# Value products in the two halves of the array's rows, and the first group's maxima in four PSUM banks

## The chip, the cores and the metric

The kernel runs as one program on one core of a Trainium2 chip. The metric is the device time of one execution in microseconds (us). Three runs of the kernel before gave 850.44, 850.53 and 852.36 us, median 850.53 us.

Engine names are those of the profile: PE is TensorE's matrix multiply, PEld its weight load, DVE is VectorE, ACT is ScalarE, POOL is GpSimd, SP is SyncE, which here only issues DMAs.

## The reference

The input x has 2048 rows of 512 numbers. Two branches are computed from it and mixed by a gate for each row:

```
g = sigmoid(sum(x * gate_w))
q, k, v = split(x @ wqkv)                       # 32 heads of 16
s = (q @ k^T) / 4, masked to 0 <= query - key < 256
a = (softmax(s) @ v) @ wo
b = (silu(x @ w_gate) * (x @ w_up)) @ w_down    # inner width 1792
out = g * a + (1 - g) * b
```

A query sees itself and the 255 keys before it. In blocks of 128 this means that a block of keys is seen by its own block of queries and by the two that follow, so by up to 384 queries.

## The kernel before, in words

The kernel holds most operands as a high and a low part (float32r) and multiplies three products (high x high, high x low, low x high) where one would do in full precision. The attention is worked group by group: a group `g` is 4 heads, and there are 8 groups.

**Start.** x is loaded and split, the values of all heads are projected in `vproj2`, and the queries and keys of groups 0 and 1 are projected. While the last 12 blocks of values are projected, the running of `first` puts in the maxima of group 0: `stage1` computes the scores of one head for one block of queries on PE (L264, heads in pairs: head `j` of a pair lies in array rows 0 to 63 or 64 to 127) and a custom DVE instruction adds the mask and takes the maximum over the keys (L266). The scores of `stage1` come from the pool `ps1`, which has two PSUM buffers (banks) handed out in turn.

**The attention loop.** Step `t` stands for group `g` and block `i` of 128 (16 steps for a group). In each step there are four parts `hd` = 0 to 3. Each part puts on PE, in this order: one score product of `stage1` for the next group (L264), one of `stage2` for this group (L301), and six products of `lanes` (L216), which are projections for a later group or early parts of the feed-forward branch. `stage2` scores go through the exponential on ACT (L303), from the pool `ps2` of two banks, into the tiles `pt`, which POOL then masks (L305, L308). From step 112 on (the last group), there is no `stage1` any more, and `stage2` runs two heads at once in parts 0 and 2.

At each fourth step, in part 1, stands a *value site*: `av` multiplies the exponentials of 4 blocks of queries (a chunk `c` of 512) with the values (L319), `evac` transposes the result out of PSUM on DVE (L329), and `finish` divides by the sum and transposes back over the next steps. There are 32 sites, `d` = 1 to 32. In `av` each product has all 128 keys of a block on the array's rows and 32 columns for a head, so the four heads of a group stand side by side in the four column groups. It runs over up to 384 queries. It sums in one bank taken from the pool `pp`.

At every second value site (steps with `i` = 8 or 0, so even `d` up to 28) `put_max` stands ahead of `av`: it transposes the maxima on PE (L276, a bank from `ps1`), DVE copies them negated into `mt` (L278), and SP moves them into the query tile, so that the score product of `stage2` subtracts them.

**The order of the work** is written out: each engine executes its instructions in the order in which the code above issues them. A PE instruction that waits for a bank holds up all that stands behind it on PE.

**The feed-forward stage** follows. For chunk `c` and slice `n` of the inner width, `hidden` takes the two inputs (kept in DRAM as `raws` and loaded as `got`, or computed on PE at L633), applies silu on ACT (L636) and multiplies on DVE (L637); `halved` splits the product into high and low (ACT L64, DVE L67); `step` multiplies with `w_down` (L82 to L84). The loop at the end of the stage keeps `halved` one slice behind `hidden`, and `step` two behind.

Of the kernel before, what the change touches and what calls it, by code (L numbers as in the profile page):

```python
# [9 lines left out]
F32 = mybir.dt.float32  # L10
# [6 lines left out]
P = 128  # L17
# [16 lines left out]
def gated_mix(ctx, tc, xT, xn, wqk, wv, wo, wgu, wd, gw, out):  # L34
# [43 lines left out]
    def mm3(ps, pairs, start=True, stop=True):  # L78

        n = len(pairs)  # L80
        for i, ((lh, ll), (rh, rl)) in enumerate(pairs):
            nc.tensor.matmul(ps, lh, rh, start=start and i == 0, stop=False)  # L82
            nc.tensor.matmul(ps, lh, rl, start=False, stop=False)  # L83
            nc.tensor.matmul(ps, ll, rh, start=False, stop=stop and i == n - 1)  # L84

    def run(gen, n=None):

# [77 lines left out]
    with ExitStack() as A:  # L165
# [87 lines left out]
        def stage1(g, qb):  # L253

            hf, b = divmod(qb, NB // 2)
            if b == 0:
                MX[g, hf] = sm.tile([P, 4, NB // 2], F32, name="mx")
            q0, k0 = qb * P, max(0, qb - 2) * P
            n = q0 + P - k0
            for hd in range(4):  # L260
                pr, j = divmod(hd, 2)
                r = slice(64 * j, 64 * j + 63)
                ps = ps1.tile([P, CH], F32, name="ps1")
                nc.tensor.matmul(ps[:, :n], QT[g % 2][pr][r, q0:q0 + P], KT[g % 2][pr][r, k0:k0 + n],  # L264
                                 start=True, stop=True)
                mx = nc.vector.tensor_tensor_reduce(out=ps[:, :n], in0=ps[:, :n], in1=mask[:, 3 * P - n:],  # L266
                                                    scale=1.0, scalar=NEG, op0=ALU.add, op1=ALU.max,
                                                    accum_out=MX[g, hf][:, hd, b:b + 1])
                if g == 0:
                    BEHIND.append(mx)  # L270
                yield

        def put_max(g, hf):
            n = NB // 2
            pt = ps1.tile([P, CH], F32, name="ps1")
            nc.tensor.transpose(pt[:4 * n, :P], MX[g, hf].rearrange("p h b -> p (h b)"), ident)  # L276
            mt = sm.tile([4 * n, P], F32R, name="mt")
            nc.vector.tensor_scalar(mt, pt[:4 * n, :P], -1.0, None, op0=ALU.mult)  # L278
            for pr in range(2):
                nc.sync.dma_start(halves_of(QT[g % 2][pr])[hf][63::64].bitcast(F32),  # L280
                                  mt[2 * pr * n:2 * (pr + 1) * n].bitcast(F32))
# [30 lines left out]

        def av(g, c):

            AV[g, c] = pp.tile([P, CH], F32, name="pb" if 4 * g + c + 1 < len(UNITS) else "pa")
            for kb in range(max(0, 4 * c - 2), 4 * c + 4):
                b0, b1 = max(kb, 4 * c), min(kb + 3, 4 * c + 4)
                for j in range(4):
                    nc.tensor.matmul(AV[g, c][32 * j:32 * j + 32, (b0 - 4 * c) * P:(b1 - 4 * c) * P],  # L319
                                     VG[4 * g + kb // 4][:, kb % 4, 17 * j:17 * j + 32],  # L320
                                     PT[g, kb, j // 2][:, j % 2, (b0 - kb) * P:(b1 - kb) * P],
                                     start=kb == max(0, 4 * c - 2), stop=kb == 4 * c + 3, skip_group_check=True)

        OT = {}

        def evac(g, c):

            OT[g, c] = osb.tile([P, CH], F32, name="ot")
            nc.vector.transpose(OT[g, c], AV[g, c])  # L329

        def finish(g, c):

# [190 lines left out]
        for t in range(G * NB + 1):  # L523
            g, i = divmod(t, NB)
            d, part = divmod(t, NSLOT)
            if part == 0:
                turns = unit(UNITS[d], t) if d < len(UNITS) else [iter(())] * NSLOT
            s1 = stage1(g + 1, i) if t < g7 else iter(())
            s2 = stage2(g, i) if t < G * NB else iter(())
            for hd in range(4):  # L530
                run(s1, 1)
                if t < g7:
                    run(s2, 1)
                elif hd % 2 == 0:
                    run(s2, 2)
                run(turns[part], 3)
                for f in AT.pop((t, hd), ()):
                    f()
                if hd == 1 and part:
                    run(FIN, 1)  # L540
                if hd == 1 and part == 0:
                    while tops:
                        put_max(*tops.pop())
                    if t:
                        ag, c = divmod(d - 1, NCH)
                        av(ag, c)
                        evac(ag, c)
                        FIN = finish(ag, c)
            if i in (7, 15) and g + 1 < G:
                tops.append((g + 1, i // 8))  # L550
            if t >= 10 and t % 4 == 2 and t + 6 < G * NB:
                load_v((t + 6) // 4)
# [11 lines left out]
    with ExitStack() as B:  # L564
# [104 lines left out]
        for c, n in seq:  # L669
# [8 lines left out]
            fresh.append((c, n, hidden(c, f)))  # L678
            for f in todo:
                f()  # L680
            if len(fresh) > 1:
                waiting.append(halved(*fresh.pop(0)))
            if c == 0 and n >= NF - 4:
                load_oc(0, n - NF + 4)
# [45 lines left out]
```

## Time and profile before

| | |
|---|---|
| median of 3 runs | 850.53 us |
| the profiled execution | 851.24 us, span 849.5 us, mean granted PE clock 0.995 |
| PE busy | 836.2 us (98%) |
| DVE busy | 507.4 us (60%) |
| ACT busy | 432.8 us (51%) |
| POOL busy | 352.2 us (41%) |
| start, with the first group's maxima | 0 to about 90 us |
| attention loop | about 90 to 619 us, PE busy all of it from 90 on |
| feed-forward stage | about 619 to 849.5 us |

The span is the time between the first and the last instruction of the profiled execution. Busy time of PE includes the time in which several products run side by side in different rows or columns of the array, counted once. The rows that the argument rests on stand in the prediction, each beside its use. A row of the timeline has its start, its duration, the engine, the line, the operation, the tiles and, in brackets, the idle time before it with what ended that. A row of a group ends in its busy time, the mean ns of one instruction, and the idle time before it.

### The profile page before, as it was taken

What the parts mean: (1) busy time and instruction counts of PE and PEld (TensorE: products, weight loads), DVE (VectorE), ACT (ScalarE), POOL (GpSimd) and SP (SyncE); (2) the same over time, 40 slices, a digit from 0 to 9 for tenths busy, and PEclk for the clock granted to TensorE, in tenths of its full rate; (3) what the DMA queues carried; (4) which work ended last, traced back from release to release, by engine and by line L of the source; (5) the groups of instructions that cost most, each with busy time, mean ns of one, the idle gap of its engine ahead of it and who ended that gap; (6) DMA issues with size and microseconds to landing.
All of it is one profiled execution on the core that took longest, in us unless ns stands there. A gap on an engine that the chain in (4) does not pass through costs nothing.

```text
span 849.5 us, 18731 instructions
## 1 busy us (share of the span) xinstructions
PE 836.2 (98%) x6934; PEld 687.3 (81%) x6934; DVE 507.4 (60%) x1382; ACT 432.8 (51%) x901; POOL 352.2 (41%) x638
## 2 busy tenths in 40 slices
PE   8999999999999999999999999999979999999998
PEld 6887878877887887887788888878858888888886
DVE  6377467667676676677577657746566254363443
ACT  6411556656565666566565655556545343243341
POOL 8611546546555645554654545456601021011020
PEclk9999999999999999999999999999989999999999
DMA  7573624534543552552453462456789454193451
GB/s 272 158 208 112 176 79 130 162 121 126 162 142 108 151 163 97 152 182 88 126 180 129 121 184 101 137 181 205 232 280 291 145 176 152 67 302 100 134 176 49
DMA packets 65995, 132.82 MB, mean 156 GB/s; under 512 B 9456, under 2 KB 14192, under 8 KB 65904
## 3 DMA queue, kind: packets, MB, share of 16 engines
q1 hardware_dynamic: 61936, 117.74, 44.3%
q0 software_dynamic: 3968, 13.90, 4.5%
q8 instruction: 54, 0.88, 0.4%
q14 instruction: 37, 0.30, 0.1%
HBM read 60.82 MB, written 45.35 MB: 125 GB/s over the span
## 4 chain that ended last, share of the span: by engine, by line
PE 93%; DVE 3%; DMA 2%; SPq 1%; issue 0%; ACT 0%
PE pa L216 23%; PE pb L216 22%; PE pb L319 9%; PE ps L84 6%; PE ps L82 6%; PE ps L83 6%; PE ps L264 6%; PE ps L301 5%; PE pa L196 2%; DVE ps L266 2%; PE pb L82 2%; PE pb L84 2%; PE pb L83 2%; PE pb L196 1%; PE pb L633 1%; PE pa L633 1%
## 5 line engine op out<-in xcount | busy, mean ns | idle before, releaser
L303 ACT ACTIVATE pt<-ps 128x384 f32<-128x384 f32 (+2 forms) x512 | 240.3, 476 | 211.4 <-PE ps L301 147.4
L266 DVE CUSTOM_DVE_ANT_0 ps<-ps,mask 128x384 f32<-128x384 f32 (+2 forms) x512 | 273.1, 539 | 97.2 <-PE ps L264 64.8
L305 POOL TENSOR_SCALAR_AFFINE_SELECT pt<-pt 128x256 f32<-128x256 f32 x256 | 111.8, 437 | 240.3 <-ACT pt L303 240.3
L264 PE MATMUL ps<-k,q 63*128 63x384 f32 (+2 forms) x512 | 168.4, 334 | 1.1
L301 PE MATMUL ps<-q,k 64*128 64x384 f32 (+2 forms) x512 | 160.3, 329 | 0.0
L216 PE MATMUL pb<-xhi,wh 64*128 64x512 f32 x512 | 111.4, 394 | 0.0
L216 PE MATMUL pa<-xhi,wh 64*128 64x512 f32 x512 | 111.1, 393 | 0.1
L216 PE MATMUL pb<-xhi,wl 64*128 64x512 f32 x512 | 110.1, 390 | 0.0
L216 PE MATMUL pb<-xlo,wh 64*128 64x512 f32 x512 | 110.0, 390 | 0.0
L216 PE MATMUL pa<-xhi,wl 64*128 64x512 f32 x512 | 109.7, 391 | 0.0
L216 PE MATMUL pa<-xlo,wh 64*128 64x512 f32 x512 | 109.6, 390 | 0.0
L264 PEld LDWEIGHTS ps<-k,q 63*128 63x128 f32 x512 | 93.7, 184 | 18.4 <-issue 5.4
L308 POOL TENSOR_SCALAR_AFFINE_SELECT pt<-pt 128x256 f32<-128x256 f32 x224 | 95.5, 426 | 0.0
L301 PEld LDWEIGHTS ps<-q,k 64*128 64x128 f32 x512 | 89.3, 184 | 7.3 <-issue 0.8
L637 DVE TENSOR_TENSOR sg<-got,sg 128x512 f32<-128x512 f32 x52 | 44.0, 846 | 64.4 <-ACT sg L636 54.0
L319 PE MATMUL pb<-pt,vg 128*32 128x256 f32 (+2 forms) x1360 | 81.5, 386 | 0.0
L319 PEld LDWEIGHTS pb<-pt,vg 128*32 128x32 f32 x1360 | 40.1, 110 | 41.0 <-issue 21.9
L266 DVE DVE_READ_ACCUMULATOR2_ANT mx<- 128x1 f32 x512 | 72.0, 141 | 0.0
L329 DVE STREAM_TRANSPOSE ot<-pb 128x512 f32<-128x512 f32 x31 | 22.2, 717 | 76.6 <-PE pb L319 76.6
L216 PEld LDWEIGHTS pb<-xhi,wh 64*128 64x128 f32 x512 | 57.1, 185 | 7.2
L216 PEld LDWEIGHTS pb<-xhi,wl 64*128 64x128 f32 x512 | 57.2, 184 | 6.3
L216 PEld LDWEIGHTS pa<-xhi,wl 64*128 64x128 f32 x512 | 56.4, 184 | 6.6
(138 smaller groups left out, 1526.5 us busy)
## 6 DMA issues: line engine op xcount, KB each, us to landing
raws<-ev SPq DMA_DIRECT2D x104, 256.0 KB
got<-raws SPq DMA_DIRECT2D x104, 256.0 KB
od<-on POOLq DMA_DIRECT2D x32, 256.0 KB, 2.4
q<-xhi SPq DMA_DIRECT2D x56, 128.0 KB
k<-xhi SPq DMA_DIRECT2D x56, 128.0 KB
raw<-wgu SPq DMA_DIRECT2D x28, 256.0 KB
vd<-vs POOLq DMA_DIRECT2D x8, 672.0 KB, 4.5
vg<-vd SPq DMA_DIRECT2D x32, 168.0 KB
```

The source lines that it names most:

```text
L82: nc.tensor.matmul(ps, lh, rh, start=start and i == 0, stop=False)
L83: nc.tensor.matmul(ps, lh, rl, start=False, stop=False)
L84: nc.tensor.matmul(ps, ll, rh, start=False, stop=stop and i == n - 1)
L216: mm = nc.tensor.matmul(ps[me], w[r], x[r], start=not second and i == 0, stop=bool(second) and i == n - 1)
L264: nc.tensor.matmul(ps[:, :n], QT[g % 2][pr][r, q0:q0 + P], KT[g % 2][pr][r, k0:k0 + n], start=True, stop=True)
L266: mx = nc.vector.tensor_tensor_reduce(out=ps[:, :n], in0=ps[:, :n], in1=mask[:, 3 * P - n:], scale=1.0, scalar=NEG, op0=ALU.add, op1=ALU.m ...
L301: nc.tensor.matmul(ps[:, :n], KT[g % 2][pr][r, k0:k0 + P], QT[g % 2][pr][r, k0:k0 + n], start=True, stop=True)
L303: BEHIND.append(nc.scalar.activation(pt[:, j, :n], ps[:, :n], AF.Exp, scale=SCALE))
L305: nc.gpsimd.affine_select(out=pt[:, :, :P], in_=pt[:, :, :P], pattern=[[0, 2], [1, P]], compare_op=ALU.is_ge, fill=0.0, base=0, channel_mu ...
L308: nc.gpsimd.affine_select(out=pt[:, :, 2 * P:], in_=pt[:, :, 2 * P:], pattern=[[0, 2], [-1, P]], compare_op=ALU.is_ge, fill=0.0, base=-1, ...
L319: nc.tensor.matmul(AV[g, c][32 * j:32 * j + 32, (b0 - 4 * c) * P:(b1 - 4 * c) * P], VG[4 * g + kb // 4][:, kb % 4, 17 * j:17 * j + 32], PT ...
L637: nc.vector.tensor_tensor(out=sg, in0=gu[1], in1=sg, op=ALU.mult)
```

## The change

1. **`av`**: a product takes 64 keys, in one half of the array's rows, and 32 columns. Each 64 keys are seen by at most 320 queries, so a product runs over at most 320 columns and not over 384. The lower halves of the blocks sum into the bank from `pp` as before, the upper halves into a second bank, taken from `ps2`. The blocks are taken in an order in which the lower half of one and the upper half of another have the same or a similar number of columns. There are twice as many products.
2. **`evac`**: ACT copies the second sum into SBUF (a tile named `on`), DVE adds the first sum to it, and then DVE transposes the sum. For chunk 0 the first 64 queries have no second sum, and are copied.
3. **`put_max`**: two products over 64 rows each, into two banks of `ps1`, and two small copies on DVE (32x64 each) where there was one of each (32x128). At the value sites it now stands behind `av` and `evac`.
4. **`stage1`**: for group 0 the second pair of heads takes its banks from `ps2`.
5. **the feed-forward loop**: the first slice is split by `halved` at once, behind its own `hidden`, and not behind that of the second slice.

```diff
@@ stage1
-                ps = ps1.tile([P, CH], F32, name="ps1")
+                ps = ps2.tile([P, CH], F32, name="ps2") if g == 0 and pr else ps1.tile([P, CH], F32, name="ps1")
@@ put_max
-            pt = ps1.tile([P, CH], F32, name="ps1")
-            nc.tensor.transpose(pt[:4 * n, :P], MX[g, hf].rearrange("p h b -> p (h b)"), ident)
             mt = sm.tile([4 * n, P], F32R, name="mt")
-            nc.vector.tensor_scalar(mt, pt[:4 * n, :P], -1.0, None, op0=ALU.mult)
+            for o in HALVES:
+                pt = ps1.tile([P, CH], F32, name="ps1")
+                nc.tensor.matmul(pt[:4 * n, :64], MX[g, hf].rearrange("p h b -> p (h b)")[o], ident[o, o],
+                                 start=True, stop=True)
+                nc.vector.tensor_scalar(mt[:, o], pt[:4 * n, :64], -1.0, None, op0=ALU.mult)
@@ av
-            AV[g, c] = pp.tile([P, CH], F32, name="pb" if 4 * g + c + 1 < len(UNITS) else "pa")
-            for kb in range(max(0, 4 * c - 2), 4 * c + 4):
-                b0, b1 = max(kb, 4 * c), min(kb + 3, 4 * c + 4)
+            AV[g, c] = (pp.tile([P, CH], F32, name="pb" if 4 * g + c + 1 < len(UNITS) else "pa"),
+                        ps2.tile([P, CH], F32, name="ps2"))
+            orders = [[4 * c + m for m in ms if 4 * c + m >= 0] for ms in ((0, 1, 2, -1, -2, 3), (0, 1, -1, 2, 3, -2))]
+            for n, kbs in enumerate(zip(*orders)):
                 for j in range(4):
-                    nc.tensor.matmul(AV[g, c][32 * j:32 * j + 32, (b0 - 4 * c) * P:(b1 - 4 * c) * P],
-                                     VG[4 * g + kb // 4][:, kb % 4, 17 * j:17 * j + 32],
-                                     PT[g, kb, j // 2][:, j % 2, (b0 - kb) * P:(b1 - kb) * P],
-                                     start=kb == max(0, 4 * c - 2), stop=kb == 4 * c + 3, skip_group_check=True)
+                    for h, (o, kb) in enumerate(zip(HALVES, kbs)):
+                        k0 = kb * P + 64 * h
+                        q0, q1 = max(k0, c * CH), min(k0 + W + 64, c * CH + CH)
+                        nc.tensor.matmul(AV[g, c][h][32 * j:32 * j + 32, q0 - c * CH:q1 - c * CH],
+                                         VG[4 * g + kb // 4][o, kb % 4, 17 * j:17 * j + 32],
+                                         PT[g, kb, j // 2][o, j % 2, q0 - kb * P:q1 - kb * P],
+                                         start=n == 0, stop=n == len(orders[0]) - 1, skip_group_check=True)
@@ evac
+            both = osb.tile([P, CH], F32, name="on")
+            lo = 0 if c else 64
+            nc.scalar.copy(both[:, lo:], AV[g, c][1][:, lo:])
+            nc.vector.tensor_tensor(out=both[:, lo:], in0=AV[g, c][0][:, lo:], in1=both[:, lo:], op=ALU.add)
+            if lo:
+                nc.vector.tensor_copy(both[:, :lo], AV[g, c][0][:, :lo])
             OT[g, c] = osb.tile([P, CH], F32, name="ot")
-            nc.vector.transpose(OT[g, c], AV[g, c])
+            nc.vector.transpose(OT[g, c], both)
@@ the attention loop, part 1 of each fourth step
-                    while tops:
-                        put_max(*tops.pop())
                     if t:
                         ag, c = divmod(d - 1, NCH)
                         av(ag, c)
                         evac(ag, c)
                         FIN = finish(ag, c)
+                    while tops:
+                        put_max(*tops.pop())
@@ the feed-forward loop
-            if len(fresh) > 1:
+            while len(fresh) > (c + n > 0):
                 waiting.append(halved(*fresh.pop(0)))
```

The change moves instructions in three places that the prediction speaks of. In the rows, `ps` is a score bank or, in the changed `av`, the second sum; `pb` is the sum from `pp`, `mx` the maxima, `mt` their negated copy, `ot` the transposed sum.

PE at the second value site (`d` = 2, step 8), before:

```order
L276 MATMUL ps_1559<-ident,mx 32x128
L319 MATMUL pb<-pt,vg 32x128 x4
L319 MATMUL pb<-pt,vg 32x256 x4
L319 MATMUL pb<-pt,vg 32x384 x8
L319 MATMUL pb<-pt,vg 32x256 x4
L319 MATMUL pb<-pt,vg 32x128 x4
L264 MATMUL ps_1592<-k_351,q_349 128x384
L301 MATMUL ps_1596<-q_86,k_88 128x384
```

and the end of the same place in the change:

```order
L330 MATMUL pb<-pt,vg 32x128
L330 MATMUL ps_1587<-pt,vg 32x128
L281 MATMUL ps_1642<-ident,mx 32x64
L281 MATMUL ps_1645<-ident,mx 32x64
L267 MATMUL ps_1650<-k_351,q_349 128x384
L306 MATMUL ps_1654<-q_86,k_88 128x384
```

The product of the maxima moved from ahead of the value products to behind them, became two, and takes both banks of `ps1` right ahead of the next score (`ps_1650`), which is given the bank of the first (`ps_1642`) again.

DVE at the same site, before:

```order
L266 ISA ps_1545,mx<-ps_1545,mask 128x384
L266 ISA mx 128x1
L278 TENSOR_SCALAR mt<-ps_1559 32x128
L329 STREAM_TRANSPOSE ot<-pb 128x512
L266 ISA ps_1592,mx<-ps_1592,mask 128x384
L266 ISA mx 128x1
```

and in the change:

```order
L342 TENSOR_TENSOR on<-pb,on 128x512
L346 STREAM_TRANSPOSE ot<-on 128x512
L283 TENSOR_SCALAR mt<-ps_1642 32x64
L283 TENSOR_SCALAR mt<-ps_1645 32x64
L269 ISA ps_1650,mx<-ps_1650,mask 128x384
L269 ISA mx 128x1
```

The copies of the maxima, which free the two banks, now stand behind the addition and the transpose of the values.

ACT at the end of the attention loop (`d` = 32), before:

```order
L303 ACTIVATE pt<-ps_9768 128x128
L473 COPY ev<-pa 128x512
L473 COPY ev<-pb 128x512 x2
L64 CAST wh<-raw 128x512
L558 ACTIVATE gate<-gate 128x16
```

and in the change:

```order
L490 COPY ev<-pa 128x512
L490 COPY ev<-pb 128x512
L341 COPY on<-ps_10652 128x512
L490 COPY ev<-pb 128x512
L64 CAST wh<-raw 128x512
L575 ACTIVATE gate<-gate 128x16
```

The copy of the second sum stands between the last two copies of kept products, the second of which SP stores as `raws` ahead of the first loads of the feed-forward stage.

More of the change, by code (lines that the diff above doesn't have):

```diff
@@ L84, in mm3 @@
             nc.tensor.matmul(ps, ll, rh, start=False, stop=stop and i == n - 1)
+    HALVES = slice(0, 64), slice(64, P)
     def run(gen, n=None):
```

## The prediction

> **What bounds the kernel now.** I read the page's busy times and its chain first, then the timeline around one value site, then the groups by shape.
>
> ```profile
> PE 836.2 (98%) x6934; PEld 687.3 (81%) x6934; DVE 507.4 (60%) x1382; ACT 432.8 (51%) x901; POOL 352.2 (41%) x638
> PE 93%; DVE 3%; DMA 2%; SPq 1%; issue 0%; ACT 0%
> ```
>
> PE is the bound: it is busy for 98% of the span and carries 93% of the chain. So time saved on PE counts in full, and so does each wait that PE is given, since PE works in the written order. DVE at 60% looks free, but what matters is how long PE needs for a given chain on DVE. The timeline shows the slack at an odd site, `d` = 3 (the score of part 2 follows at 141.28, that of part 0 of the next step at 143.13):
>
> ```profile
> 138.55 2.80 PE L319 MATMUL pb<-pt,vg 128*32 128x128 f32 x48
> 141.28 0.44 PE L264 MATMUL ps<-k,q 63*128 63x384 f32 x1
> 141.42 0.72 DVE L329 STREAM_TRANSPOSE ot<-pb 128x512 f32<-128x512 f32 x1 [2.85 <-PE pb L319]
> 141.85 0.49 ACT L303 ACTIVATE pt<-ps 128x384 f32<-128x384 f32 x1 [2.76 <-PE ps L301]
> 142.06 0.53 DVE L266 CUSTOM_DVE_ANT_0 ps<-ps,mask 128x384 f32<-128x384 f32 x1
> 142.51 0.13 DVE L266 DVE_READ_ACCUMULATOR2_ANT mx<- 128x1 f32 x1
> 143.13 0.34 PE L264 MATMUL ps<-k,q 63*128 63x384 f32 x1
> ```
>
> The value products end at E = 138.55 + 2.80 = 141.35. `ps1` has two banks in turn, so the score at 143.13 needs the bank of the score at 141.28, which DVE gives back with the `mx` row, at 142.51 + 0.13 = 142.64. The slack is 143.13 - 142.64 = 0.49 us. Whatever lengthens the way from E to that row by more than 0.49 us stops PE.
>
> **The value products.** 48 records for the 24 products of a chunk: each goes over its columns twice.
>
> ```profile
> L319 PE MATMUL pb<-pt,vg 128*32 128x384 f32 x496 | 45.9, 488 | 0.0
> L319 PE MATMUL pb<-pt,vg 128*32 128x128 f32 x432 | 22.2, 278 | 0.0
> L319 PEld LDWEIGHTS pb<-pt,vg 128*32 128x32 f32 x1360 | 40.1, 110 | 41.0 <-issue 21.9 <-ACT ev L473 3.3 <-ACT pt L303 2.9
> ```
>
> 256 columns more take 488 - 278 = 210 ns, 0.82 ns a column. Before, a head has 128+256+384+384+256+128 = 1536 columns in a chunk (1152 in chunk 0), and the four heads run beside each other: 2 x 1536 x 0.82 = 2.52 us, and 0.21 us remain of the 2.73 from 138.55 to the next score. The change has 320+320+256+192+128+64 = 1280 columns in each half (1024 in chunk 0). If the halves run beside each other, as the two row halves do elsewhere (six half products of 512 columns in 0.69 us, in a row of the part on the first maxima), and the step of 64 columns takes the 110 ns of a weight load for each pass, this is 2 x (1216 x 0.82 + 110) + 210 = 2.42 us. It saves 0.31 us at 24 sites, and 2 x 128 x 0.82 = 0.21 at the 8 sites of chunk 0: **-9.1 us**. The bounds: -11.9 if the 64 columns take 52 ns, 0 if half of the overlap is lost.
>
> The Trainium skill ("TensorEngine Tiling (Array Packing)", Instruction Overhead) has about 60 cycles as the floor of a product, which a product of 64 columns would be just above. By it that step would cost the 52 ns, and the sum would be 2.8 us lower; the weight loads of 110 ns in this trace speak for the longer value.
>
> **The chain behind an odd site.** The evacuation gains a copy on ACT and an addition on DVE, all between E and the next `mx`.
>
> ```profile
> L473 ACT COPY ev<-pb 128x512 f32<-128x512 f32 x64 | 37.4, 585 | 0.5 <-ACT ev L473 0.5
> L637 DVE TENSOR_TENSOR sg<-pb,sg 128x512 f32<-128x512 f32 x4 | 2.8, 690 | 26.8 <-PE pb L633 26.8
> L637 DVE TENSOR_TENSOR sg<-got,sg 128x512 f32<-128x512 f32 x52 | 44.0, 846 | 64.4 <-ACT sg L636 54.0 <-DMA got<-raws 10.3
> L278 DVE TENSOR_SCALAR mt<-ps 32x128 fp32r<-32x128 f32 x16 | 4.5, 279 | 8.2 <-PE ps L276 8.2
> ```
>
> ACT wakes 0.13 us after PE (the score that starts at 141.28 with 0.44 ends at 141.72, ACT begins at 141.85) and is idle at E, as the bracket of its row shows. Copy, of the same shape as L473: E + 0.13 + 0.58 = E + 0.71. DVE wakes after 0.05 and adds in 0.69 (the row with one PSUM input; 0.85 as the upper bound, the mean of the other): E + 1.45. Transpose 0.72, as in L329's row: E + 2.17. The maximum up to its `mx` row takes 142.64 - 142.06 = 0.58: E + 2.75, and with 0.05 for PE's wake E + 2.80. PE would be there at 143.13, E + 1.78. So PE stands still for 1.0 us, once: afterwards DVE needs about 0.6 us for each score and PE brings one each 0.86 (0.17 for a pair of scores, 0.69 for six half products, rows below). Bounds 0.75 and 1.4 (a slower addition, and some stalls behind the divisions). Fourteen odd sites have `stage1` behind them (d = 1 to 27): **+14.0 us**. While PE stands, the projections behind the score stand too.
>
> **The even sites.** `put_max` now takes both banks of `ps1` behind the value products, and its copies on DVE stand behind the addition and the transpose (order rows above). So the score of part 2 itself, at once behind E, waits for the first copy. Before:
>
> ```profile
> 155.18 0.22 PE ps L276
> 155.39 2.73 PE pb L319 x48
> 158.12 0.25 PE ps L264
> ```
>
> Only 0.22 us of PE went to it, and none to waiting. Now: E + 2.17 from above, 0.22 for a copy of half of L278's columns (279 ns; its whole is the upper bound), 0.05 to wake: E + 2.44, where the score stood at 141.28, E - 0.07. That is 2.51 us, and 0.22 is gone from ahead: 2.29 net, bounds 2.0 and 2.8. DVE has nothing left to do then, so no second stall. Thirteen sites (d = 2 to 26): **+29.8 us**. At step 0 `put_max` has no value site, but the next score waits for its copy: +0.4.
>
> **The last group.** There is no `stage1`, but the second sum holds one of the two banks of `ps2`, and two scores follow at once:
>
> ```profile
> 614.37 0.22 PE L301 MATMUL ps<-q,k 64*128 64x128 f32 x1
> 614.46 0.22 PE L301 MATMUL ps<-q,k 64*128 64x128 f32 x1
> ```
>
> They started 0.09 apart; now the second waits for the copy, E + 0.76, against about E + 0.05. 0.7 us at d = 28 to 31: **+2.8 us** (bounds 1.5 and 3.5).
>
> **The first group's maxima.** Here the change should gain. The chain of waits, one block of queries in the start:
>
> ```profile
> 46.11 0.57 DVE ps L266
> ...
> 47.30 0.44 PE ps L264
> 47.74 1.16 PE pb L216 x10
> 48.97 0.57 DVE ps L266
> ...
> 130.13 0.69 PE pa L216 x6
> 130.82 0.16 PE ps L264
> 130.98 0.01 PE ps L301
> ```
>
> With two banks PE and DVE wait for each other, and a block takes 48.97 - 46.11 = 2.86 us. With four banks PE can run at its own pace: 12 turns of 12 pairs are 144 pairs of projections over 16 blocks, 9 each, at 0.69 / 3 = 0.23 us, and two pairs of scores at 0.17: 2.41 us. DVE needs at most 4 x 0.57 = 2.3 and keeps up. 0.45 us at the 14 blocks of full width is 6.3; I take **-6.0 us** for some waits on a late weight (bounds -3 and -8).
>
> **The start of the feed-forward stage.** The split of the first slice no longer stands behind a load of `w_down`:
>
> ```profile
> 616.22 1.08 ACT L473 COPY ev<-pb 128x512 f32<-128x512 f32 x2 [0.51 <-ACT ev L473]
> 617.32 2.70 DMA raws<-ev
> 620.20 0.32 SPq L622
> 625.08 0.69 DVE L637 TENSOR_TENSOR sg<-got,sg 128x512 f32<-128x512 f32 x1 [3.38 <-ACT sg L636]
> 626.48 0.50 PE L82 MATMUL ps<-q,hh 128*128 128x512 f32 x1 [1.81 <-ACT hh L64]
> 629.59 0.68 DVE L67 TENSOR_TENSOR hl<-sg,hh 128x512 fp32r<-128x512 f32 x1
> 630.33 0.80 PE L84 MATMUL ps<-q,hl 128*128 128x512 f32 x1 [3.12 <-DVE hl L67]
> ```
>
> That alone would bring L84 forward by about 3 us. But the last ACT copy of kept products, ended at 617.30, now stands behind the copy of the last value site, whose products end at 618.5: 618.5 + 0.13 + 0.58 + 0.58 = 619.8, 2.5 us later, and the store and the loads follow it on SP's queue. So the product at 625.08 starts at 627.6; addition of 0.69, the split on ACT (about 0.65) and on DVE (0.7) bring L84 to 629.7: **-0.6 us** (bounds -4 if the loads are not delayed, +3 if the later steps lack `hl`).
>
> **The sum**: -9.1 + 14.0 + 29.8 + 0.4 + 2.8 - 6.0 - 0.6 = +31.3 us, from the profiled 851.24 to 882.5. That execution is 0.7 us above the median of 850.53; against the median I forecast **882 us**.
>
> **The rivals.**
>
> *The halves don't run beside each other* in these products of two passes. Nothing in this trace has a product of two passes in half of the rows; the half products of L216 and the score pairs do overlap. Then a chunk takes 4 x 1280 x 0.82 + 0.21 = 4.4 us (3.4 in chunk 0), +1.7 and +1.3, 51 us instead of -9: about 942 us. Chance 0.05.
>
> *The waits cool the clock.* In the row of stretches (stretches of 3 us; the third number from the right is the granted clock) PE had some 5 us of idle time, and ran at half speed after it:
>
> ```profile
> 625.00:628.00 3.00, 0.73 (x2) 0.30 (x2) 1.29 (x2) 2.19 (x5) 0.00 (x0) 1.00 1.04 397
> 628.00:631.00 3.00, 0.67 (x2) 0.57 (x3) 2.44 (x5) 0.69 (x2) 0.00 (x0) 0.72 0.70 257
> 631.00:634.00 3.00, 3.00 (x9) 2.32 (x8) 2.93 (x6) 1.17 (x2) 0.00 (x0) 0.50 0.82 279
> 633.69 0.43 PE ps L82
> 637.62 0.23 PE ps L82
> ```
>
> A dozen products at 0.43 instead of 0.23 us cost 2.4 us. If the even sites' 2.4 us did the same, 13 x 2.4 = 31 us more: 913. Against it: the first 1.81 us of idle time left the clock at 1.00. The Trainium skill ("TensorE: Matmul & The Clock Gate", HAM oscillation) puts the limit at about 3.4 us of idle time, and by that rule these waits leave the clock alone. Chance 0.06.
>
> *Not slower: the score behind a site does not wait.* If the banks were given so that the score of part 2 and the one two parts later don't need what stands behind the transpose (the maxima in banks of their own would do it), only the gains and the last group are left: 851.2 - 9.1 - 6.0 - 0.6 + 2.8 = 838, 837.6 against the median. For it: PE has no wait at any site now, and DVE idles for 2.85 us ahead of each transpose. Against it: `ps1` has two banks, and the rows of the order give both to the maxima. It decides once the way from E to the bank's return is under 1.78 us (odd) and the copy leaves the way (even). If waits of about 0.5 us were left at the 27 sites, their 13.5 us would cancel the 12.9 that is left of the gains (9.1 + 6.0 + 0.6 - 2.8), and nothing could be told. Chance of the rival 0.05, of the cancelling 0.02.
>
> **How the numbers follow.** The forecast has 0.82. Adding the low bounds gives -11.9 + 10.5 + 26 + 0.4 + 1.5 - 8 - 4 = +14.5, 865; the high ones 0 + 19.6 + 36.4 + 0.4 + 3.5 - 3 + 3 = +60, 910. The range is 865 to 910, which leaves out the rivals and little else. A change under 0.3% can hardly be told from none here. Faster has the not-slower rival's 0.05, within 0.3% the cancelling's 0.02, slower the rest, 0.93.
>
> **What would show it.** In the profile after: waits of PE on DVE `mt` of 2 to 2.5 us (13 times) and on DVE `mx` of about 1 us (14 times), which weigh most; value products of about 2.4 us to a site; DVE's addition at 0.69; a block of the first maxima at 2.4 us; and a clock of 1.00 through the loop. I'm wrong if PE stays busy at 98% through the attention loop, or if the value products take over 4 us.

## The result and the profile after

The change makes the kernel slower: 902.53 us, median of 5 runs (901.24 to 903.31), against 851.27 us for the kernel before (5 runs, 850.44 to 852.36). The ratio is 1.0603, 95% interval 1.0584 to 1.0621. The forecast was 882 us with a range of 865 to 910: the sign and the places were right, and 20 us were missing. The profiled execution took 903.31 us with a span of 901.6 us, 52.1 us above the 849.5 of before, at a granted clock of 0.977 on average, where it was 0.995.

The page of the kernel after, busy times and the chain:

```profile
PE 844.4 (94%) x8390; PEld 707.5 (78%) x8390; DVE 526.2 (58%) x1438; ACT 452.9 (50%) x933; POOL 352.8 (39%) x638
PE 84%; DVE 6%; DMA 4%; ACT 3%; issue 2%; SPq 0%; POOL 0%; DVEq 0%; ACTq 0%; POOLq 0%
```

PE's share of the chain fell from 93% to 84%; DVE, DMA and ACT took its place. The loss is in the attention loop. In the view of stretches (length, then busy time of PE, PEld, DVE, ACT and POOL with the number of instructions, granted clock, DMA share, GB/s), first of before, then of after:

```profile
105.00:600.00 495.00, 495.00 (x5105) 406.23 (x5102) 327.81 (x1028) 295.53 (x652) 265.45 (x534) 1.00 0.45 142
```

```profile
100.00:600.00 500.00, 457.27 (x5829) 382.69 (x5827) 318.75 (x1019) 282.87 (x610) 236.13 (x478) 0.97 0.39 120
```

Before, PE never stood still there. After, it stands for 42.7 us of 500, and its clock is 0.97. Both matter. PE's waits in the kernel after (us in total, times, longest) say for what it stood:

```profile
PE ps L267 <- DVE mt L283: 29.5, 14, 2.3
PE ps L267 <- DVE mx L269: 11.0, 14, 0.9
PE ps L306 <- ACT on L341: 5.3, 7, 1.7
PE ps L82 <- ACT hh L64: 4.3, 1, 4.3
```

The first two rows are the even sites (13, and step 0) and the 14 odd sites of the prediction. An even site, `d` = 2, in the timeline:

```profile
120.32 0.22 PE L281 MATMUL ps<-ident,mx 64*32 64x64 f32 x1
120.56 0.58 ACT L341 COPY on<-ps 128x512 f32<-128x512 f32 x1 [2.59 <-PE ps L281]
121.17 0.69 DVE L342 TENSOR_TENSOR on<-pb,on 128x512 f32<-128x512 f32 x1 [3.18 <-ACT on L341]
121.90 0.71 DVE L346 STREAM_TRANSPOSE ot<-on 128x512 f32<-128x512 f32 x1
122.54 0.30 DVE L283 TENSOR_SCALAR mt<-ps 32x64 fp32r<-32x64 f32 x2
122.77 0.44 PE L267 MATMUL ps<-k,q 63*128 63x384 f32 x1 [2.23 <-DVE mt L283]
```

PE finishes the product of the maxima at 120.54 and stands until 122.77, behind ACT's copy, DVE's addition, the transpose, and only then the small copies that give the banks back. An odd site, `d` = 3:

```profile
140.91 0.44 PE L267 MATMUL ps<-k,q 63*128 63x384 f32 x1
...
141.63 0.69 DVE L342 TENSOR_TENSOR on<-pb,on 128x512 f32<-128x512 f32 x1 [3.17 <-ACT on L341]
...
142.36 0.71 DVE L346 STREAM_TRANSPOSE ot<-on 128x512 f32<-128x512 f32 x1
...
143.44 0.13 DVE L269 DVE_READ_ACCUMULATOR2_ANT mx<- 128x1 f32 x1
143.63 0.44 PE L267 MATMUL ps<-k,q 63*128 63x384 f32 x1 [0.72 <-DVE mx L269]
```

The `mx` row ends at 143.57, and the score that needs its bank starts 0.06 later, after a stop of 0.72 us.

Two things in this profile were not in the forecast's sum. **The clock.** Here are two pairs of neighbouring stretches of the kernel after, around the stop at site 12 and around that at site 14:

```profile
307.97:311.38 3.41, 1.15 (x50) 0.99 (x36) 1.79 (x5) 0.63 (x2) 0.12 (x1) 1.00 0.02 5
311.38:314.79 3.41, 3.41 (x21) 3.17 (x19) 1.05 (x6) 2.42 (x5) 1.59 (x3) 0.50 0.55 185
345.51:348.93 3.42, 1.72 (x84) 1.34 (x68) 1.02 (x2) 0.58 (x1) 0.05 (x1) 1.00 0.02 5
348.93:352.34 3.41, 2.88 (x26) 2.49 (x28) 2.48 (x9) 2.26 (x5) 0.82 (x3) 1.00 0.22 84
```

In the first stretch PE stands for 2.26 us, and the whole next stretch runs at half clock. In the third the same kind of stop is cut in two by the edge at 348.93; 1.70 us of it lie in the one stretch, the rest in the next, and the clock stays. There are ten stretches at half clock in the attention loop, each 3.41 us long, behind the stops at the even sites 2, 4, 6, 8, 10, 12, 16, 20, 24 and 26. Beside the three even sites without one, each costs 1.5 to 1.6 us: 15.4 us in all.

**A store.** At some sites of chunk 0 ACT could not start its copy. Site 13, from the chain of waits in order of time (start, length), and from the timeline:

```profile
323.65 5.92 DMA od<-on
```

```profile
329.67 0.53 ACT L341 COPY on<-ps 128x448 f32<-128x448 f32 x1 [3.39 <-DMA od<-on]
330.25 0.44 PE L306 MATMUL ps<-q,k 64*128 64x384 f32 x1 [0.71 <-ACT on L341]
332.30 0.44 PE L267 MATMUL ps<-k,q 63*128 63x384 f32 x1 [0.91 <-DVE mx L269]
```

`evac` now puts the second sum into a tile named `on`, the name of the tile from which `finish` of the site before is stored, and their pool has one buffer for that name. The chain has 5.92 us for that store, and 6.39 and 5.87 at sites 17 and 21. The copy waits for it, and starts 1.2 to 1.7 us later behind the products than at the other sites of chunk 0. Sites 13, 17 and 21 lose 4.2 us in this way, and site 29 some 1.4.

### The profile page after: what moved, and what is told of

It reads as the page before. It is cut to its first block, busy times and chain, and to the rows that moved or that the text cites. A ratio compares the mean times of both kernels' runs of the same rounds, so it can differ in the third digit from the quotient of the medians.

```text
span 901.6 us, 21679 instructions
## 1 busy us (share of the span) xinstructions
PE 844.4 (94%) x8390; PEld 707.5 (78%) x8390; DVE 526.2 (58%) x1438; ACT 452.9 (50%) x933; POOL 352.8 (39%) x638
## 4 chain that ended last, share of the span: by engine, by line
PE 84%; DVE 6%; DMA 4%; ACT 3%; issue 2%; SPq 0%; POOL 0%; DVEq 0%; ACTq 0%; POOLq 0%
PE pb L218 21%; PE pa L218 20%; PE ps L82 6%; PE ps L84 6%; PE ps L83 6%; PE pb L330 6%; PE ps L267 5%; PE ps L306 4%; DVE on L342 2%; DMA od<-on 2%; ACT on L341 2%; PE pa L198 2%; PE pb L83 2%; PE pb L82 2%; PE pb L84 2%
## 5 line engine op out<-in xcount | busy, mean ns | idle before, releaser
L306 PE MATMUL ps<-q,k 64*128 64x384 f32 (+2 forms) x512 | 169.2, 340 | 5.3 <-ACT on L341 5.3
L218 PE MATMUL pa<-xhi,wh 64*128 64x512 f32 x512 | 115.5, 405 | 0.1
L218 PE MATMUL pa<-xhi,wl 64*128 64x512 f32 x512 | 115.0, 406 | 0.0
L218 PE MATMUL pa<-xlo,wh 64*128 64x512 f32 x512 | 113.7, 401 | 0.0
L306 PEld LDWEIGHTS ps<-q,k 64*128 64x128 f32 x512 | 96.8, 191 | 13.8 <-ACT on L341 7.4
L342 DVE TENSOR_TENSOR on<-pb,on 128x512 f32<-128x512 f32 (+1 forms) x31 | 20.9, 674 | 98.7 <-ACT on L341 98.7
L330 PE MATMUL ps<-pt,vg 64*32 64x320 f32 (+4 forms) x1408 | 75.0, 346 | 0.0
L330 PE MATMUL pb<-pt,vg 64*32 64x320 f32 (+3 forms) x1360 | 73.9, 350 | 0.0
L330 PEld LDWEIGHTS pb<-pt,vg 64*32 64x32 f32 x1360 | 46.4, 106 | 28.2 <-ACT pt L308 9.9
L218 PEld LDWEIGHTS pa<-xhi,wl 64*128 64x128 f32 x512 | 59.5, 191 | 6.9
```

Of the source, the lines that this page charges most:

```text
L218: mm = nc.tensor.matmul(ps[me], w[r], x[r], start=not second and i == 0, stop=bool(second) and i == n - 1)
L306: nc.tensor.matmul(ps[:, :n], KT[g % 2][pr][r, k0:k0 + P], QT[g % 2][pr][r, k0:k0 + n], start=True, stop=True)
L330: nc.tensor.matmul(AV[g, c][h][32 * j:32 * j + 32, q0 - c * CH:q1 - c * CH], VG[4 * g + kb // 4][o, kb % 4, 17 * j:17 * j + 32], PT[g, kb, ...
```

## The experiments

The kernel before beside the runs below had medians of 851.0 to 851.1 us, with 852.2 for the two single runs.

### The maxima ahead of the value products again

```diff
@@ the attention loop, part 1 of each fourth step (against the change)
+                    while tops:
+                        put_max(*tops.pop())
                     if t:
                         av(ag, c)
                         evac(ag, c)
                         FIN = finish(ag, c)
-                    while tops:
-                        put_max(*tops.pop())
```

> The change with the maxima's products back ahead of the value products at each site; all else as changed. Theory (PE waits for the DVE chain, and the long still times of 2.25 us at the even sites are what lowers the clock): the even sites become like the odd ones, 13 x (2.07 - 0.58) = 19 us less, and the 10 stretches at half clock (15 us) go: about 868 us, granted clock back at about 0.995, no wait of PE on mt over 0.3 us. Rival (the value products in 64 x 32 tiles count as little activity and lower the clock themselves): the stretches stay, about 883 us, clock about 0.978.

Measured: 867.67 us (865.82 to 869.6), ratio 1.0194 (1.0175 to 1.0214). PE's waits in it:

```profile
PE ps L267 <- DVE mx L269: 18.9, 27, 0.9
```

Moving one loop brings 35 us back. The wait on `mt` shrinks to 0.3 us at step 0, and the even sites now wait for `mx` like the odd ones: 27 times, 0.7 us each. No stretch of the attention loop runs at half clock, and the granted clock is 0.996. PE's busy time falls by 12.9 us and its idle time by 24.6, so a large part of the idle time and the whole of the half clock in the loop hung on that place. A stop of 0.7 us leaves the clock alone.

### The transpose behind the copies of the maxima

```diff
@@ evac (against the change)
-            OT[g, c] = osb.tile([P, CH], F32, name="ot")
-            nc.vector.transpose(OT[g, c], both)
+            def turned():
+                OT[g, c] = osb.tile([P, CH], F32, name="ot")
+                nc.vector.transpose(OT[g, c], both)
+            return turned
@@ the attention loop
-                        evac(ag, c)
-                        FIN = finish(ag, c)
+                        turned = evac(ag, c)
                     while tops:
                         put_max(*tops.pop())
+                    if turned:
+                        turned()
+                        FIN = finish(ag, c)
```

> The change with DVE's transpose of the values moved behind the two copies of the maxima, which still stand behind the addition. The still time of PE at the even sites should fall by the transpose, from 2.25 to about 1.55 us: 13 x 0.71 = 9 us less. If the clock only falls when PE stands for about 2 us or more, the 10 stretches at half clock go too: about 878 us. If 1.5 us are enough for it, they stay: about 893 us.

Measured: 875.3 us (874.72 to 877.18), ratio 1.0291 (1.0273 to 1.0309). The waits, and two stretches around site 2:

```profile
PE ps L267 <- DVE mt L283: 20.1, 14, 1.5
...
PE ps L306 <- ACT on L341: 1.8, 5, 0.5
```

```profile
120.00:124.00 4.00, 2.49 (x83) 2.12 (x66) 2.07 (x6) 1.23 (x3) 0.00 (x0) 1.00 0.02 4
124.00:128.00 4.00, 4.00 (x40) 3.48 (x38) 3.35 (x11) 2.98 (x7) 2.95 (x5) 1.00 0.39 139
```

The stops are 0.7 us shorter at each even site, 9.4 us together, but the kernel gains 27. Stops of 1.5 us are followed by no half clock at all, and the wait on `on` went from 5.3 to 1.8 us. That is 9.4 + 15.4 + 3.5 = 28.3, near the 28.6 between the spans (901.6 and 873.0). The place and the work are the same in both kernels, so here the half clock goes with the length of the stop.

### The store one step earlier

```diff
@@ finish (against the change)
             nc.vector.transpose(on, OT[g, c])
-            yield
             nc.gpsimd.dma_start(od[g, :, c * CH:(c + 1) * CH], on)
```

> The change with the store of the finished values one step (some 3.5 us) earlier on POOL's queue, at once behind the second transpose. Theory: at four sites of chunk 0 ACT's copy of the second sum waits for that store, because both use the one buffer of the tile on; PE loses about 5.5 us to it. So about 897 us, and no wait of ACT on the store is left. Rival: the copy is late there for another reason, 902 us and the same late copies.

Measured: 902.33 us (901.4 to 902.88), ratio 1.06 (1.0584 to 1.0616), where about 897 was expected. PE's wait on `on` shows that the store no longer holds up the copy:

```profile
PE ps L306 <- ACT on L341: 1.3, 4, 0.3
```

PE waits for `on` only in the last group now, 4.0 us less in all. But twelve even sites, not ten, are followed by half clock: the work was shifted against the edges of the clock's stretches. At 1.54 us each, two more are 3.1 us, most of what the store gave. This follows from the count of stretches and was not isolated further.

### How long a stop has to be

Part of the transpose (its first 256 or 384 columns) stays ahead of the copies of the maxima and the rest follows them (the attention loop calls it there, as in the run with the whole transpose behind), so that the stop lies between the 1.5 us and the 2.25 us above.

```diff
@@ evac (against the change)
-            nc.vector.transpose(OT[g, c], both)
+            nc.vector.transpose(OT[g, c][:, :256], both[:, :256])     # the other run: 384
+
+            def turned():
+                nc.vector.transpose(OT[g, c][:, 256:], both[:, 256:])
+            return turned
...
```

> The change with half of the values' transpose (256 of 512 columns) behind the copies of the maxima: PE stands for about 1.9 us at each even site. In the traces so far the clock fell only at the edge of stretches of 3.413 us in which PE had been idle for 2.15 us or more (all such stretches), and not at 1.83 or less. If that is the rule and the limit lies above 1.9, no stretch at half clock in the loop: about 880 us. If it lies below, about ten of them: 895 us.

> The same with 384 of the 512 columns ahead of the copies: PE stands for about 2.07 us. With the limit below this, stretches at half clock follow wherever a whole stop falls into one stretch of 3.413 us, and none where the edge cuts it: about 897 us; with the limit above it, none: about 882 us. If the clock falls with something else than idle time in a stretch, stops of the same length would show it at random places.

Measured, one run each and so without an interval: 891.07 us with 256 columns, 904.82 with 384. The wait of the first, and a half clock in it with the stretch ahead:

```profile
PE ps L267 <- DVE mt L283: 26.0, 14, 2.0
```

```profile
410.17:413.58 3.41, 1.45 (x41) 1.17 (x29) 2.22 (x7) 1.00 (x3) 0.00 (x0) 1.00 0.00 0
413.58:416.99 3.41, 3.41 (x20) 2.96 (x18) 1.37 (x6) 2.03 (x5) 2.01 (x3) 0.50 0.42 159
```

With stops of 1.97 to 1.99 us six of the thirteen even sites are followed by half clock, each behind a stretch with 1.96 to 1.99 us of idle time. No stretch of its loop with 1.84 us or less was. (The expectation has no drop at 1.83 us or less in the traces so far; the run of the next section with the feed-forward loop alone has one, at 1.83 us.) With stops of up to 2.12 us (384 columns) twelve stretches of the loop run at half clock, the time is above both that were expected, and a simple limit fails. These two pairs go the wrong way round:

```profile
422.01:425.42 3.41, 1.49 (x76) 1.19 (x60) 1.24 (x3) 0.59 (x1) 0.00 (x0) 1.00 0.02 5
425.42:428.83 3.41, 3.23 (x30) 2.87 (x32) 2.48 (x11) 2.36 (x6) 1.17 (x3) 1.00 0.33 126
480.05:483.46 3.41, 1.74 (x12) 0.97 (x11) 2.36 (x7) 2.30 (x5) 1.03 (x3) 1.00 0.00 1
483.46:486.87 3.41, 3.41 (x20) 2.84 (x20) 2.06 (x8) 0.98 (x2) 1.93 (x3) 0.50 0.35 108
```

An idle time of 1.92 us left the clock alone, and one of 1.67 us did not (a third case had 1.50 us, and two stretches at half clock behind it). So the idle time in a stretch, as the records give it, decides nearly always but not alone; what else counts stays open.

### Each of the two side gains by itself

On the kernel before, only the banks of the first group's maxima:

```diff
@@ stage1 (against the kernel before)
-                ps = ps1.tile([P, CH], F32, name="ps1")
+                ps = ps2.tile([P, CH], F32, name="ps2") if g == 0 and pr else ps1.tile([P, CH], F32, name="ps1")
```

> The kernel before with one part of the change: the second pair of heads of group 0 takes its banks from the other pool. Theory of the prediction: a block falls from 2.86 to 2.41 us and the whole by 6.0 us, 845 us; the profile of the full change suggests 4.9 us of it, 846 us. Rival (the start is bound by the transfers, and the time comes back before the loop): 850 to 851 us.

And on the kernel before, only the feed-forward loop:

```diff
@@ the feed-forward loop (against the kernel before)
-            if len(fresh) > 1:
+            while len(fresh) > (c + n > 0):
                 waiting.append(halved(*fresh.pop(0)))
```

> The kernel before with one part of the change: the split of the first slice directly behind its own hidden step. Here no copy of the value site delays the loads. The prediction had this as its lower bound, L84 3 us earlier and the gain up to 4 us: 847 to 848 us. Rival (the next split, or the cooled clock, takes it back): 850 to 851 us.

Measured: 846.92 us (846.27 to 849.08), ratio 0.9956 (0.9942 to 0.997), and 849.35 us (847.93 to 851.81), ratio 0.998 (0.9969 to 0.9991). The first is worth 4.1 us, the second 1.7. In the second, the timeline of the first products with `w_down`, and two stretches around them:

```profile
626.42 0.50 PE L82 MATMUL ps<-q,hh 128*128 128x512 f32 x1 [1.83 <-ACT hh L64]
627.14 0.73 PE L84 MATMUL ps<-q,hl 128*128 128x512 f32 x1
```

```profile
623.83:627.24 3.41, 1.58 (x7) 0.67 (x5) 1.53 (x3) 2.64 (x5) 0.00 (x0) 1.00 1.02 380
627.24:630.65 3.41, 3.41 (x8) 2.64 (x9) 2.55 (x5) 1.80 (x4) 0.00 (x0) 0.50 0.69 261
```

L84 comes at 627.14, 3.2 us ahead of the 630.33 of before, as worked out. The stop of 1.83 us lies whole in one stretch, and the next runs at half clock; before, two stretches did. So the lead first grows: the product of L82 that started at 638.14 before starts at 634.46, 3.7 us ahead. Later it shrinks, to 2.7 us (670.98 against 673.65), which is also the difference of the two profiled spans. Two new waits on `hl`, of 0.3 and 0.4 us, are part of that; the rest was not followed.

### The same products, with the evacuation spread

Against the change, the maxima stand ahead of the products, the store goes one step earlier, and the addition and the transpose are put behind the maxima of parts 2 and 3:

```diff
@@ evac (against the change): ACT's copy at once, the other two when they are called
+            def added():
+                nc.vector.tensor_tensor(out=both[:, lo:], in0=AV[g, c][0][:, lo:], in1=both[:, lo:], op=ALU.add)
...
+            def turned():
+                OT[g, c] = osb.tile([P, CH], F32, name="ot")
+                nc.vector.transpose(OT[g, c], both)
+            return added, turned
@@ the attention loop, in each part hd
                 run(s1, 1)
+                DUE.pop(hd, int)()
...
-                        evac(ag, c)
+                        DUE.update(zip((2, 3), evac(ag, c)))
```

> The maxima's products back ahead of the value products, the store one step earlier, DVE's addition moved behind the maximum of part 2 and the transpose behind that of part 3; the rest as changed. Theory: with the chain no longer ahead of the next maxima PE has no wait at the sites with stage 1, and only the gains are left: -7.6 (value products), -4.5 (first maxima), -0.9 (feed-forward), +2 (last group), about 840 us, faster than before. Rival (DVE hasn't the time for one more instruction of 0.69 us at each site, and lags behind instead): waits of PE on mx of half a microsecond at each site, 850 us or more.

Measured: 841.72 us (841.19 to 843.99), ratio 0.9894 (0.9877 to 0.9911). PE's row of its page, and site 3 in its timeline:

```profile
PE 824.3 (98%) x8390; PEld 699.6 (83%) x8390; DVE 516.8 (62%) x1438; ACT 448.4 (53%) x933; POOL 354.5 (42%) x638
```

```profile
137.02 0.69 DVE L344 TENSOR_TENSOR on<-pb,on 128x512 f32<-128x512 f32 x1
137.04 0.34 PE L267 MATMUL ps<-k,q 63*128 63x384 f32 x1
...
137.91 0.33 PE L267 MATMUL ps<-k,q 63*128 63x384 f32 x1
138.09 0.71 DVE L350 STREAM_TRANSPOSE ot<-on 128x512 f32<-128x512 f32 x1
```

The copy, the addition and the transpose are all there, as long as before. But each stands behind a maximum that PE needs sooner, and PE brings the scores 0.87 us apart (137.04, 137.91) with no idle time ahead. So it was the order of the work, and not its amount, that made the change slow.

Without the two side gains, the value products and their spread evacuation alone:

```diff
@@ stage1 (against the kernel of the last run)
-                ps = ps2.tile([P, CH], F32, name="ps2") if g == 0 and pr else ps1.tile([P, CH], F32, name="ps1")
+                ps = ps1.tile([P, CH], F32, name="ps1")
@@ the feed-forward loop
-            while len(fresh) > (c + n > 0):
+            if len(fresh) > 1:
```

> The spread order of the earlier run (maxima ahead, addition and transpose of the values behind the next two maxima, early store) without the two parts tried alone: first group in two banks, feed-forward loop as before. So the value products in row halves alone, with their evacuation hidden: 7.6 us less for the products, 1.6 us more in the last group, a little more at the end of the loop: about 846 us. If the change of order had given the gain and not the halves, 851 us.

Measured: 848.46 us (847.43 to 849.81), ratio 0.9972 (0.9961 to 0.9982): 2.6 us by the medians, 3.8 between the profiled spans (849.5 and 845.7), for products that take 7.6 us less. Its waits name most of the rest:

```profile
PE ps L82 <- ACT hh L64: 4.8, 1, 4.8
PE ps L84 <- DVE hl L67: 2.0, 1, 2.0
```

The start of the feed-forward stage waits 4.8 + 2.0 = 6.8 us, where before it was 1.81 + 3.12 = 4.9 (the brackets of L82 and L84 in the prediction): ACT's copy of the second sum at site 32 stands ahead of what is stored and loaded there (the next run moves it). With 1.3 us for `on` in the last group, the same as with the early store, that is 3.2 of the 3.8 us that are missing between the spans.

Both can be taken away: the second sum of the last sites from `ps1`, which has no scores left then, and the last kept product's copy ahead of the last value site.

```diff
@@ av (against the spread version)
-                        ps2.tile([P, CH], F32, name="ps2"))
+                        ps1.tile([P, CH], F32, name="ps1") if 4 * g + c + 1 >= 28 else ps2.tile([P, CH], F32, name="ps2"))
@@ the attention loop, ahead of av
+                        if t == G * NB:
+                            for f in AT.pop((t, 2), ()):
+                                f()
```

> The spread order with two more edits: in the last group the second sum takes its bank from the pool of the maxima, which is free then, and at the last site ACT's copy of the second sum stands behind the copies of the kept products. The score products of the last group no longer wait (0.33 us at four sites, 1.3 us) and the loads of the feed-forward stage start some 0.7 us earlier or more: 838 to 840 us, against 841.7. If neither wait was on the path: 841 to 842 us.

Measured: 838.99 us (837.17 to 841.7), ratio 0.9862 (0.9841 to 0.9882), faster than both kernels. The wait on `on` has gone from its list, and the one on `hh` is 2.3 us, where the spread version had 4.1. What each of the two edits brought was not measured.

## Why the prediction was right, and where it missed

The spans differ by 52.1 us, where the sum had 31.3. Each site's interval to the next was compared between the two traces, and the half clock's share taken out of the even ones by the three sites that have none:

| step | predicted, us | measured, us |
|---|---|---|
| value products, 32 sites | -9.1 | -7.6 |
| chain behind an odd site, 14 | +14.0 | +12.0 (11.0 of waits on `mx`, about 1 not assigned) |
| even sites, 13 | +29.8 | +30.2 |
| the half clock | 0 (a rival) | +15.4 |
| late store at sites 13, 17, 21 | not seen | +4.2 |
| start and first maxima, with step 0 | -5.6 | -4.5 |
| last group | +2.8 | +3.4 (1.4 of it the store) |
| start of the feed-forward stage | -0.6 | -0.9 |
| sum | +31.3 | +52.2 |

The time lies inside the range of 865 to 910 because the range is wide: its bounds were made without the half clock and the store, which are 19.6 us of the 52.2 at the sites named.

**The even sites** came out as worked: 2.32 us each against 2.29. The chain copy, addition, transpose, small copy was built from rows of the same shapes, and the moved product of the maxima was followed past all of them.

**The value products**: the two halves do run beside each other, so the rival of 942 us falls. (Its 3.4 us for chunk 0 left out the 0.21 us; with them it is 3.6, and 943 in all.) A site's products take 2.55 us from the first start to the last end, 2.80 before. That is 0.25 us, not 0.31 (0.20 in chunk 0). Two groups of the kernel after, and site 3:

```profile
L330 PE MATMUL pb<-pt,vg 64*32 64x320 f32 x496 | 40.3, 435 | 0.0
L330 PE MATMUL ps<-pt,vg 64*32 64x128 f32 x192 | 12.0, 280 | 0.0
```

```profile
140.28 0.22 PE L330 MATMUL pb<-pt,vg 64*32 64x64 f32 x1
...
140.39 0.27 PE L330 MATMUL pb<-pt,vg 64*32 64x128 f32 x1
...
140.71 0.27 PE L330 MATMUL ps<-pt,vg 64*32 64x128 f32 x1
```

192 columns less save 435 - 280 = 155 ns, 0.81 a column, as taken. But three terms were mis-sized, and they nearly cancel. The step of 64 columns was taken at 110 ns a pass. Its two passes, sixteen starts, take 0.11 us together (140.28 to 140.39), 55 ns each: the lower bound of 52 came, 0.11 us better than the sum. The Trainium skill ("TensorEngine Tiling (Array Packing)", Instruction Overhead) has about 60 cycles as the floor of a product, by which the prediction put this step at 52 ns; the trace agrees with that. What was gained there was nearly given back by the 128 columns behind it: from 140.39 to the next score at 140.91 are 0.52 us, where the working has 0.42 (two passes of 0.105 and the 0.21 carried over). Why their sixteen starts spread over 0.32 us is not shown. And ahead of that step the passes follow each other at 0.84 ns a column (0.269 us for 320), not 0.82, which with a longer first pass (0.293 us) makes 0.07 us. That is +0.10 - 0.11 + 0.07 = 0.06 us less gain a site.

**The odd sites**: a stop of 0.72 us against 1.0. Of the difference, half is the chain: it ended at E + 2.65 instead of E + 2.80 (143.63, with E = 140.98), since ACT began 0.03 us behind E (at 141.01), not 0.13. The other half is PE, which came 0.15 us later than the E + 1.78 of the working: 143.63 - 0.72 = 142.91. A difference of two long paths carries the errors of both.

**The clock** is the step that failed: the sum has it at nothing. The rival had the mechanism, at a chance of 0.06 and 2.4 us for each of 13 sites; it came at 10 sites with 1.54 us each. The working had half clock behind some 5 us of idle time, and 1.81 us as leaving the clock at 1.00. Both were read across stretches of 3 us. Here is the trace of before at the edges of the clock's own stretches of 3.41 us:

```profile
625.89:629.30 3.41, 0.73 (x2) 0.30 (x2) 1.23 (x3) 1.58 (x3) 0.00 (x0) 1.00 1.05 405
629.30:632.71 3.41, 2.38 (x6) 1.90 (x7) 3.38 (x7) 1.36 (x3) 0.00 (x0) 0.50 0.66 228
```

The stop of 1.81 us ended at 626.48, so the edge at 625.89 cut it into 1.2 and 0.6 us. In the first stretch shown PE stands for 3.41 - 0.73 = 2.68 us, in two pieces, and the next runs at half clock. So the trace on which the forecast rests already showed that 2.7 us within one stretch were enough, and it showed nothing for a whole stop of 1.81 us. Such a stop, of 1.83 us, came in the run with the feed-forward loop alone, with half clock behind it (in the attention loops 1.83 and 1.84 us left the clock alone). By the Trainium skill ("TensorE: Matmul & The Clock Gate", HAM oscillation), whose limit is about 3.4 us of idle time, these stops would have left the clock alone; the trace doesn't agree, with ten drops behind stops of 2.2 to 2.3 us.

**The late store** was not in the working, which lets the copy start as soon as the products end. Who else uses the one buffer of `on` was not followed. The store holds up the copy only at the four sites of chunk 0 named above.

**The first maxima**: the blocks run at PE's pace, as forecast: the first scores of three blocks in turn start at 47.26, 49.72 and 52.17, some 2.45 us apart, with 2.41 worked out. Most of what is missing of the 6.0 is one wait, 0.9 us, for ACT, which was held by a weight's load:

```profile
62.52 0.62 ACT L64 CAST wh<-raw 128x512 fp32r<-128x512 f32 x1 [11.78 <-DMA raw<-wgu]
63.68 0.50 PE L218 MATMUL pa<-wvh,xhi 64*128 64x512 f32 x1 [0.89 <-ACT vs L389]
```

By itself this part brought 4.1 us, inside its bounds of 3 and 8.

**The last group and the feed-forward start** came near their sums by other terms. The plain stop in the last group is about 0.3 us a site, not 0.7, and the store at site 29 made up for it, with some 0.7 us not assigned; that the term came near was luck. At the feed-forward start the delay of ACT's copy was there as worked, with a wait of 4.3 us on `hh`.

**Not slower**: this rival (838 us) needed the banks' return to be independent of the transpose. The spread versions did just that by order, not by banks, and reached 841.72 and 838.99. Its price was near; its condition does not hold in the change.

## What to carry to other kernels

Ask of each instruction added on a helper engine what that engine owes the bound engine next, and put it behind that debt: here the same copies, additions and transposes, in another order around the same maxima and stores, made the difference between 902.5 and 841.7 us. Price a stop of the bound engine twice, once for its length and once for the clock behind it. Don't take a shorter stop in the trace as proof for a longer one, and count idle time between the edges of the clock's stretches, which the start of any half clock in the trace gives away. When a change takes a tile by a name already in use, follow the last reader of that buffer, which may be a store.

## What the hardware showed

- The clock drops came in whole stretches of 3.41 us. Their starts in the kernel after (123.65, 161.19, 198.74, 236.29, 273.83, 311.38, 386.47, 461.57, 536.66 and 574.21) are multiples of 3.413 us apart: 37.55 us is 11 of them, 75.1 is 22. The Trainium skill ("TensorE: Matmul & The Clock Gate", Part 1) speaks of a free-running window of 4096 cycles, about 3.4 us; the trace agrees with that.
- About 2 us of idle time within one such stretch were enough. In the attention loops, every stretch with 1.96 to 2.26 us of it was followed by half clock (37 stretches, in the change and three of its variants); those with 1.92 us or less were not, but for two in the run with 384 columns (1.67 and 1.50 us). In the run with the feed-forward loop alone 1.83 us were enough, at the start of the feed-forward stage. A stop cut by an edge escaped (sites 14, 18 and 22). What decides below 1.96 us stays open.
- Because of these edges, a gain of a few us elsewhere can be lost without any wait in the profile: with the store one step earlier the waits fell by 4 us, the drops rose from 10 to 12, and the time stayed.
- Products of two passes in 64 rows and 32 columns run eight at a time: eight starts within 0.05 us, then 0.269 us to the next eight with 320 columns, 0.84 ns a column, and 55 ns with 64 columns. The 128-column products right behind the 64-column ones started over 0.32 us, in sixteen starts.
